# Layer 1's block products in three PSUM chains per half, read between the products

## The chip, the cores and the metric

One core of a Trainium2 chip runs the whole kernel in one launch. The metric is device time in microseconds (us), lower is better. The core's engines work side by side, each on its own instruction queue in order: TensorE (PE) multiplies matrices into PSUM banks, VectorE (DVE), ScalarE (ACT) and GpSimd (POOL) do element work, and SyncE (SP) issues transfers (DMA). An instruction waits until the semaphores it names have been raised by others, and everything queued behind it on its engine waits too.

## The reference

Three stages follow each other: attention with a decay, a mixture of 8 experts over its output, and a two-layer network with a leaky activation.

```python
x = attention(q, k, v, f)          # 4 x 8 heads, 576 tokens, 64 wide -> (2304, 512)

# mixture of experts: N, D, E, F = 2304, 512, 8, 1024
P = exp(x @ w_gate - max); 8 times: rows and columns of P are normalised
for e in range(E):
    h = np.maximum(x @ w1[e], 0.0)
    out += P[:, e:e + 1] * (h @ w2[e])

# two layers: d_model, d_ff = 512, 2048
h = x @ w_in
return np.maximum(0.01 * h, h) @ w_out
```

## The kernel before

**Stages.** Up to about 388 us the kernel does attention, with parts of the first experts mixed in, and the normalisation of the gate. From then on a main loop runs over 56 *groups* (`keys`). The 2304 tokens are three *parts* of 768, and the hidden width is cut in groups of 512 columns: 16 for the experts (g 0 to 15, two per expert), 4 for the last two layers (g 16 to 19). Part 0 begins at g 4, then come parts 1 and 2 with 16 groups each, then four groups of the last layers for each part.

**Precision.** Each float32 operand is split into a high half (`wh`, `xh`, `hh`), rounded by ACT, and a low half (`wl`, `xl`, `hl`), the rest by subtraction. Weights' low halves are GpSimd's (`w_split`, L202). A product is three matmuls, high by high, high by low and low by high.

**Layer 1.** A group's x @ w is done by a fast scheme with seven block products in place of eight, in two *halves* s = 0, 1 of 128 hidden columns each per block. The blocks of x (`b11` to `b22`) and of w (`a11` to `a22`) enter by sums and differences: `t1` to `t4` of x are made once per part, `s1` to `s4` of w in each group (`w1_events`: `s1` is an addition on DVE, L940, the `sub` are subtractions, L944, both working on the weights' buffer `wr`). A product (`prod`, L1027 to L1029) is six matmuls of 384 columns into a PSUM bank of its own, from a pool `ps1` of five. The output blocks are sums of products: c11 = p1 + p2; with u2 = p1 + p6 and u3 = u2 + p7: c22 = u3 + p5, c21 = u3 + p4, c12 = u2 + p5 + p3. ACT copies p1 and p5 from PSUM to SBUF (`keep`, L1034). DVE adds c11, u2, u3, c12 and c21 (L1044), GpSimd adds v = p5 + u2 and c22 = p5 + u3 (L1044, tiles `v` and `p`). c11 and u2 lie in one tile, `ct`. Then each c is made into its high half on ACT (`high`, L1062) and its low half on DVE (`low`, L1067 and, in the last layers, after a leaky activation, L1048, by L1070).

**Layer 2.** For the group before, six blocks l of 128 tokens each, twelve matmuls of 512 columns (L1130 to L1132) into another pool of three banks; DVE adds each to the sum over experts, weighted by the gate (`l2_add`, L1144). Scaling of the sums of the first experts at the loop's start is L1210.

**Order.** The program is a list of events with planned times (`at`); all events are sorted by time, after their `need` has put each behind those it depends on, and issued in that order. So the plan sets the order on every engine; the chip sets the times. `STEP_T` holds corrections to planned times, in the first group for every step. The products of a half come as p1 p6 p5 p2 p7 p3 p4 (`SET`). A pattern of 20 letters mixes products (p) and layer-2 blocks (l): `PAIRS` in the second and third group and the last, with the blocks in three runs, `THREES` in the 52 others, with two runs of three. The first group has products alone. `op_events` makes the operands of x anew at five turns, from one part to the next and at the groups of the last layers (`OPS` lists name, place, planned times of load, high and low half, and the engine of the low half, L823). Weights of a group come by two transfers, issued when the buffers `wr` are free.

Of the kernel before, what the change touches and what calls it, by code (L numbers as in the profile page):

```python
# [8 lines left out]
F32 = mybir.dt.float32  # L9
# [3 lines left out]
AF = mybir.ActivationFunctionType  # L13
ALU = mybir.AluOpType
# [121 lines left out]
def moe_kernel(ctx, tc, qT, kT, v, fg, w_gate, w1, w2, w_in, w_out, out):  # L136
# [192 lines left out]
    with ExitStack() as actx:  # L329
# [366 lines left out]
        def at(n, t, fn, *args):  # L696
            todo.append((n + t, len(todo), fn, args))
# [71 lines left out]
    fps[0] = ps2  # L769
    HB = 2 * KC - 1  # L770
    ht = late.tile([P, 2 * HB, TB], F32R, tag="xp", name="ht")
    ct = late.tile([P, 2, TB], F32, tag="xq", name="ct")
    hpb, owner, l2done = list(range(HB)), {}, set()


# [100 lines left out]
    def op_load(key, name, place):  # L876
# [136 lines left out]

    HT = {}

    def l1_events(prev, key, s, fin):

        part, g = key
        ps, tmp = {}, {}

        def prod(name, wn, xn):
            o = ps1.tile([P, 512], F32, tag="l1", name="ps1")[:, :TB]
            hi, lo = W1[key][wn]
            xh, xl = xo[xn]
            fs = slice(s * P, (s + 1) * P)
            for k in range(2):
                nc.tensor.matmul(o, hi[:, k, fs], xh[:, k, :], start=(k == 0), stop=False)  # L1027
                nc.tensor.matmul(o, hi[:, k, fs], xl[:, k, :], start=False, stop=False)  # L1028
                nc.tensor.matmul(o, lo[:, k, fs], xh[:, k, :], start=False, stop=(k == 1))  # L1029
            ps[name] = o  # L1030

        def keep(name):
            tmp[name] = tp.tile([P, TB], F32, tag=name, name=name, bufs=2 if name == "p1" else 1)
            nc.scalar.activation(tmp[name], ps.pop(name), AF.Copy)  # L1034

        def add(name, a, b, eng, into=None):
            a = ps.pop(a) if a in ps else tmp[a]
            if into:
                tmp[name] = tmp[into]
            elif name in ("c11", "u2"):  # L1040
                tmp[name] = ct[:, int(name == "u2"), :]
            else:
                tmp[name] = tp.tile([P, TB], F32, tag=name, name=name)
            eng.tensor_tensor(tmp[name], a, tmp[b], ALU.add)  # L1044

        def leaky(name):
            c = tmp[name]
            nc.scalar.activation(c, c, AF.Prelu, alpha=0.01)  # L1048

        def high(name, fh, th):  # L1050
            if th:
                hh = hpa.tile([P, TB], F32R, tag="hh", name="hh")
                hl = hpa.tile([P, TB], F32R, tag="hl", name="hl")
            else:
                i = hpb.pop(0)

                assert i not in owner or (owner[i], TPB - 1) in l2done, (key, owner[i])
                owner[i] = key
                hpb.append(i)
                hh, hl = ht[:, 2 * i, :], ht[:, 2 * i + 1, :]  # L1060
            tmp[fh, th] = (hh, hl)
            nc.scalar.activation(hh, tmp[name], AF.Relu if g < GE else AF.Copy)  # L1062

        def low(name, fh, th):
            hh, hl = HT.setdefault(key, {})[fh * 2 + s, th] = tmp[fh, th]
            if g < GE:
                nc.vector.scalar_tensor_tensor(  # L1067
                    hl, tmp[name], 0.0, f(hh), ALU.max, ALU.subtract)
            else:
# [21 lines left out]
        r11 = max(r1, fin["p2"]) + 0.5 + HOP
        last = (key, 0) if s else (prev, 1) if prev else None
        before = [(last[0], f"{last[1]} low c11")] if last else []
        at(r11 - 0.5, key, f"{s} c11", add, "c11", "p2", "p1", v,
           need=[(key, f"{s} keep p1"), (key, f"{s} p2"), *before])
        out_events("c11", 0, 0, r11)
        ru = max(r1, fin["p6"]) + 0.5 + HOP
        before = [(last[0], f"{last[1]} {n}") for n in ("v", "u3")] if last else []
        at(ru - 0.5, key, f"{s} u2", add, "u2", "p6", "p1", v,
           need=[(key, f"{s} keep p1"), (key, f"{s} p6"), *before])  # L1100
        step(fin["p5"] + HOP, "keep p5", keep, "p5", need=["p5"])
        r5 = fin["p5"] + 0.4 + HOP
        rv = max(r5, ru) + 1.0 + HOP
# [6 lines left out]
        out_events("c22", 1, 1, r22 + (LATE if g >= GE or g == GE - 1 and s else 0.0))  # L1110
        r3 = max(rv, fin["p3"]) + 0.5 + HOP
        step(r3 - 0.5, "c12", add, "c12", "p3", "v", v, "v", need=["v", "p3"])
        out_events("c12", 0, 1, r3)
        r4 = max(r22, fin["p4"]) + 0.5 + HOP
        step(r4 - 0.5, "c21", add, "c21", "p4", "u3", v, "u3", need=["c22", "p4"])
        out_events("c21", 1, 0, r4)
# [148 lines left out]
    for ki, key in enumerate(keys):  # L1265
# [130 lines left out]
```

## Time and profile before

| | us |
|---|---|
| median of the runs | 2147.82 |
| lowest, highest | 2146.76, 2148.51 |
| span of the profiled execution | 2145.7 |
| PE busy | 2111.3 |
| DVE busy | 1703.4 |
| POOL busy | 1374.1 |
| ACT busy | 1023.9 |

The span is from the first to the last instruction of one profiled execution. Busy is the time in which an engine works on an instruction; where one engine is busy all the time, the others' idle time costs nothing. The page has further the span in 40 slices, the groups of instructions by source line with their mean time, and the chain of waits that ended last. The trace behind it gives the same for any stretch: waits of an engine with what released them, and every instruction with its start.

### The profile page before, as it was taken

What the parts mean: (1) busy time and instruction counts of PE and PEld (TensorE: products, weight loads), DVE (VectorE), ACT (ScalarE), POOL (GpSimd) and SP (SyncE); (2) the same over time, 40 slices, a digit from 0 to 9 for tenths busy, and PEclk for the clock granted to TensorE, in tenths of its full rate; (3) what the DMA queues carried; (4) which work ended last, traced back from release to release, by engine and by line L of the source; (5) the groups of instructions that cost most, each with busy time, mean ns of one, the idle gap of its engine ahead of it and who ended that gap; (6) DMA issues with size and microseconds to landing.
All of it is one profiled execution on the core that took longest, in us unless ns stands there. A gap on an engine that the chain in (4) does not pass through costs nothing.

```text
span 2145.7 us, 31647 instructions
## 1 busy us (share of the span) xinstructions
PE 2111.3 (98%) x11134; PEld 1899.7 (89%) x11134; DVE 1703.4 (79%) x2545; ACT 1023.9 (48%) x2291; POOL 1374.1 (64%) x1039
## 2 busy tenths in 40 slices
PE   7999999999999999999999999999999999999999
PEld 6888888889999998999999998999999998989988
DVE  6799975788888877888888877888888885766754
ACT  7888863443334343333434353343434346554642
POOL 4666653776666677666656666665666576676662
PEclk9999999999999999999999999999999999999999
DMA  4555523323232324223222323223222233332310
GB/s 133 169 154 146 143 86 108 123 94 98 91 101 89 130 99 145 91 91 105 85 96 94 125 77 133 96 82 99 91 91 99 91 123 104 135 106 101 110 61 30
DMA packets 128063, 226.75 MB, mean 106 GB/s; under 512 B 11968, under 2 KB 45504, under 8 KB 127904
## 3 DMA queue, kind: packets, MB, share of 16 engines
q1 hardware_dynamic: 127904, 224.73, 32.6%
q8 instruction: 88, 1.44, 0.3%
q14 instruction: 71, 0.58, 0.1%
HBM read 189.24 MB, written 30.70 MB: 103 GB/s over the span
## 4 chain that ended last, share of the span: by engine, by line
PE 91%; DVE 5%; issue 1%; ACT 1%; POOL 1%; DMA 1%; SPq 0%; DVEq 0%; POOLq 0%; ACTq 0%
PE ps L1131 14%; PE ps L1132 14%; PE ps L1130 14%; PE ps L1027 12%; PE ps L1029 12%; PE ps L1028 12%; PE ps_pv L570 3%; PE ps L241 3%; PE ps L267 2%; PE ps_t L534 2%; PE ps_s L482 1%; PE ps_s L483 1%; POOL wl L202 1%; DVE ptl L550 1%; DMA wr<-in_w_dram 0%
## 5 line engine op out<-in xcount | busy, mean ns | idle before, releaser
L202 POOL TENSOR_TENSOR wl<-wr,wh 128x512 fp32r<-128x512 f32 x608 | 873.6, 1449 | 394.0 <-ACT wh L201 286.1
L201 ACT ACTIVATE wh<-wr 128x512 fp32r<-128x512 f32 x608 | 362.6, 621 | 461.7 <-DVE wr L944 243.9
L1027 PE MATMUL ps<-xh_t,wh 128*128 128x384 f32 x896 | 301.4, 336 | 3.5 <-DVE u L1044 2.3
L1029 PE MATMUL ps<-xh_t,wl 128*128 128x384 f32 x896 | 300.9, 336 | 0.0
L1028 PE MATMUL ps<-xl_t,wh 128*128 128x384 f32 x896 | 300.1, 335 | 0.0
L1044 POOL TENSOR_TENSOR p<-p,u 128x384 f32<-128x384 f32 x112 | 134.3, 1199 | 252.2 <-DVE u L1044 247.8
L1131 PE MATMUL ps<-wl,hh 128*128 128x512 f32 x672 | 262.6, 391 | 0.4 <-POOL wl L202 0.4
L1132 PE MATMUL ps<-wh,hl 128*128 128x512 f32 x672 | 262.7, 391 | 0.0
L1132 PE MATMUL ps<-wh,ht 128*128 128x512 f32 x672 | 262.6, 391 | 0.0
L1131 PE MATMUL ps<-wl,ht 128*128 128x512 f32 x672 | 262.4, 391 | 0.0
L1130 PE MATMUL ps<-wh,hh 128*128 128x512 f32 x672 | 262.0, 390 | 0.0
L1130 PE MATMUL ps<-wh,ht 128*128 128x512 f32 x672 | 262.0, 390 | 0.0
L1027 PE MATMUL ps<-xh_b,wh 128*128 128x384 f32 x672 | 224.8, 335 | 1.0 <-DVE v L1044 1.0
L1029 PE MATMUL ps<-xh_b,wl 128*128 128x384 f32 x672 | 224.6, 334 | 0.1
L1028 PE MATMUL ps<-xl_b,wh 128*128 128x384 f32 x672 | 224.5, 334 | 0.0
L1144 DVE SCALAR_TENSOR_TENSOR acc<-ps,prob,acc 128x512 f32<-128x512 f32 x252 | 184.7, 744 | 35.5 <-PE ps L1132 35.4
L1027 PEld LDWEIGHTS ps<-xh_t,wh 128*128 128x128 f32 x896 | 168.2, 188 | 8.8 <-DVE u L1044 3.2
L1062 ACT ACTIVATE hh<-v 128x384 fp32r<-128x384 f32 x112 | 58.5, 522 | 241.3 <-DVE v L1044 241.3
L1028 PEld LDWEIGHTS ps<-xl_t,wh 128*128 128x128 f32 x896 | 168.2, 188 | 4.1
L1029 PEld LDWEIGHTS ps<-xh_t,wl 128*128 128x128 f32 x896 | 168.1, 188 | 0.3 <-POOL wl L202 0.3
L1132 PEld LDWEIGHTS ps<-wh,ht 128*128 128x128 f32 x672 | 126.1, 188 | 26.5
L1132 PEld LDWEIGHTS ps<-wh,hl 128*128 128x128 f32 x672 | 126.1, 188 | 26.5
(177 smaller groups left out, 4649.4 us busy)
## 6 DMA issues: line engine op xcount, KB each, us to landing
wr<-in_w_dram SPq DMA_DIRECT2D x200, 512.0 KB
wr<-wf SPq DMA_DIRECT2D x48, 512.0 KB
rq<-in_qT_dram SPq DMA_DIRECT2D x64, 144.0 KB
rk<-in_kT_dram SPq DMA_DIRECT2D x64, 144.0 KB
cv<-in_w_in_dram SPq DMA_DIRECT2D x32, 256.0 KB
wf<-cv SPq DMA_DIRECT2D x64, 128.0 KB
cv<-in_w_out_dram SPq DMA_DIRECT2D x32, 256.0 KB
xt<-xr SPq DMA_DIRECT2D x20, 384.0 KB
```

The source lines that it names most:

```text
L201: nc.scalar.activation(hv, src, AF.Copy)
L202: nc.gpsimd.tensor_tensor(lv, src, f(hv), ALU.subtract)
L241: nc.tensor.matmul(ps, w_[:, fs], x_[k][:, xs], start=(x == 0), stop=(x == 11))
L570: nc.tensor.matmul(ps[:, a - ra:rb - ra], vp, s[:KV[j], o:o + rb - a], start=(x == 0), stop=(x == len(todo) - 1))
L1027: nc.tensor.matmul(o, hi[:, k, fs], xh[:, k, :], start=(k == 0), stop=False)
L1028: nc.tensor.matmul(o, hi[:, k, fs], xl[:, k, :], start=False, stop=False)
L1029: nc.tensor.matmul(o, lo[:, k, fs], xh[:, k, :], start=False, stop=(k == 1))
L1044: eng.tensor_tensor(tmp[name], a, tmp[b], ALU.add)
L1130: nc.tensor.matmul(ps, hh[:, ts], hi, start=(c == 0), stop=False)
L1131: nc.tensor.matmul(ps, hh[:, ts], lo, start=False, stop=False)
L1132: nc.tensor.matmul(ps, hl[:, ts], hi, start=False, stop=(c == FC - 1))
L1144: nc.vector.scalar_tensor_tensor(a, ps, pe, a, ALU.mult, ALU.add)
```

## The change

A half's seven products go into three banks that stay open: chain A takes p1 and p2, B takes p6, p7 and p4, C takes p5 and p3. Only a chain's first product starts it (`start`); the later ones add to what lies there. Between products the bank is read: k1 (copy of p1, on ACT) from A; u2 = B + k1, u3 = B + k1 and c21 = B + k1 from B after p6, p7 and p4; c22 = C + u3 and c12 = C + u2 from C after p5 and p3. c11 is A itself; its high and low half read PSUM. Of a half's work the additions c11 and v and the copy of p5 are gone, and c22 is now DVE's. The products p2, p7, p3 and p4 have a `need` on the read before them (k1, u2, c22, u3). The tile `ct` is gone; k1, u2 and u3 have two buffers each.

The order of products is a new table for both halves together (a digit for the half, one for the product), one for the first group and one for the others, and one pattern with layer 2's blocks in runs of three, two and one in all groups. The corrections of `STEP_T` for the first group's additions and halves are gone. In `OPS` the operand t3 takes the place of b11 and is loaded and split ahead of b21.

```diff
-    ("b21", "b21", None, -8.4, -6.6, "v"),
-    ("t3", "b11", -9.0, -2.5, 0.0, "p"),
+    ("t3", "b11", -12.0, -8.4, -6.6, "p"),
+    ("b21", "b21", None, -1.5, 0.5, "v"),
...
+    CHAIN = dict(p1="A", p2="A", p6="B", p7="B", p4="B", p5="C", p3="C")
...
         def prod(name, wn, xn):
-            o = ps1.tile([P, 512], F32, tag="l1", name="ps1")[:, :TB]
+            ch = CHAIN[name]
+            if ch not in ps:
+                ps[ch] = ps1.tile([P, 512], F32, tag="l1", name="ps1")[:, :TB]
+            o = ps[ch]
+            first, last = name in ("p1", "p6", "p5"), name in ("p2", "p4", "p3")
...
-                nc.tensor.matmul(o, hi[:, k, fs], xh[:, k, :], start=(k == 0), stop=False)
...
-            nc.scalar.activation(tmp[name], ps.pop(name), AF.Copy)
...
+                nc.tensor.matmul(o, hi[:, k, fs], xh[:, k, :], start=first and k == 0, stop=False,
+                                 skip_group_check=True)
...
+        def keep():
+            tmp["k1"] = tp.tile([P, TB], F32, tag="k1", name="k1", bufs=2)
+            nc.scalar.activation(tmp["k1"], ps["A"], AF.Copy)
...
-            eng.tensor_tensor(tmp[name], a, tmp[b], ALU.add)
+                tmp[name] = tp.tile([P, TB], F32, tag=name, name=name, bufs=2)
+            nc.vector.tensor_tensor(tmp[name], ps[ch], tmp[b], ALU.add)
...
+            if name == "c11" and g < GE:
+                tmp[name] = ps["A"]
...
+        after = {"p2": ["k1"], "p7": ["u2"], "p3": ["c22"], "p4": ["u3"]}
         for name in SET:
-            at(fin[name] - TPROD, key, f"{s} {name}", prod, name, WN[name], XN[name])
+            at(fin[name] - TPROD, key, f"{s} {name}", prod, name, WN[name], XN[name],
+               need=[(key, f"{s} {n}") for n in after.get(name, ())])
...
-        step(rv - 1.0, "v", add, "v", "p5", "u2", p, need=["keep p5", "u2"])
-        step(r22 - 1.0, "c22", add, "c22", "p5", "u3", p, "p5", need=["v", "u3"])
+        step(r2 - 0.5, "u2", add, "u2", "B", "k1", need=["k1", "p6"])
+        step(r3 - 0.5, "u3", add, "u3", "B", "k1", need=["u2", "p7"])
+        step(r22 - 0.5, "c22", add, "c22", "C", "u3", "u3", need=["u3", "p5"])
+        step(r12 - 0.5, "c12", add, "c12", "C", "u2", "u2", need=["c22", "p3"])
+        step(r21 - 0.5, "c21", add, "c21", "B", "k1", "k1", need=["u3", "p4"])
...
-    PAIRS, THREES = "pppllpppppllpppppllp", "pppplllppppppplllppp"
-    SET = ["p1", "p6", "p5", "p2", "p7", "p3", "p4"]
+    ORDER = "01 06 05 07 02 11 03 04 16 15 17 12 13 14".split()
+    FIRST_ORDER = "01 06 05 11 07 02 16 03 04 15 17 12 13 14".split()
+    PATTERN = "ppplllpppppppllpplpp"
+    SET = ["p1", "p6", "p5", "p7", "p2", "p3", "p4"]
```

What this does to the order of instructions is shown at three places. The first is DVE's queue in the first group, from the addition s1 of the next group's weights on (`s1`, `wr`: weights; `u3`, `ct`, `v`: sums of products; `ht`, `hl`: low halves). Before:

```order
L940 TENSOR_TENSOR s1_5530<-wr_5501,wr_5503 128x512
L1044 TENSOR_TENSOR v_5524<-ps1_5537,v_5524 128x384
L1044 TENSOR_TENSOR u3_5545<-ps1_5516,ct_4931 128x384
L1067 SCALAR_TENSOR_TENSOR ht_4930<-ct_4931,ht_4930 128x384
L944 TENSOR_TENSOR wr_5501<-wr_5501 128x2x256
L944 TENSOR_TENSOR wr_5501<-s1_5530,wr_5501 128x2x256
L1044 TENSOR_TENSOR u3_5545<-ps1_5553,u3_5545 128x384
L1067 SCALAR_TENSOR_TENSOR hl_5570<-p5_5495,hh_5569 128x384
L1044 TENSOR_TENSOR ct_4931<-ps1_5588,p1_5586 128x384
```

After (c22 is the second addition into `u3`; `u2_5574` is u2 of half 1; c12 and c21 are the additions into `u2_5493` and `k1`):

```order
L927 TENSOR_TENSOR s1_5526<-wr_5499,wr_5501 128x512
L1036 TENSOR_TENSOR u3_5538<-ps1_5469,k1_5476 128x384
L931 TENSOR_TENSOR wr_5499<-wr_5499 128x2x256
L1036 TENSOR_TENSOR u3_5538<-ps1_5486,u3_5538 128x384
L931 TENSOR_TENSOR wr_5499<-s1_5526,wr_5499 128x2x256
L1064 SCALAR_TENSOR_TENSOR ht_4930<-ps1_5450,ht_4930 128x384
L1064 SCALAR_TENSOR_TENSOR hl_5560<-u3_5538,hh_5559 128x384
L1036 TENSOR_TENSOR u2_5574<-ps1_5542,k1_5520 128x384
L1036 TENSOR_TENSOR u2_5493<-ps1_5486,u2_5493 128x384
L931 TENSOR_TENSOR wr_5501<-wr_5501,wr_5499 128x2x256
L1036 TENSOR_TENSOR k1_5476<-ps1_5469,k1_5476 128x384
```

The addition c22, for which p3 now waits, stands behind s1, u3 and one subtraction, and a second and a third subtraction stand ahead of the additions of half 1.

The second place is DVE's queue in the second group, from its s1 on (`acc`: sums of layer 2's blocks; `xr`: x). Before:

```order
L940 TENSOR_TENSOR s1_5749<-wr_5713,wr_5715 128x512
L1144 SCALAR_TENSOR_TENSOR acc4_96<-ps2_5731,prob_104,acc4_96 128x512
L944 TENSOR_TENSOR wr_5713<-wr_5713 128x2x256
L1044 TENSOR_TENSOR ct_4931<-ps1_5759,p1_5684 128x384
L826 TENSOR_TENSOR xr_5581<-xr_5581 128x2x384
L1044 TENSOR_TENSOR u3_5789<-ps1_5768,ct_4931 128x384
L1067 SCALAR_TENSOR_TENSOR ht_4930<-ct_4931,ht_4930 128x384
L944 TENSOR_TENSOR wr_5713<-s1_5749,wr_5713 128x2x256
L1044 TENSOR_TENSOR v_5723<-ps1_5782,v_5723 128x384
L1044 TENSOR_TENSOR u3_5789<-ps1_5794,u3_5789 128x384
```

After:

```order
L927 TENSOR_TENSOR s1_5729<-wr_5699,wr_5701 128x512
L1129 SCALAR_TENSOR_TENSOR acc4_96<-ps2_5711,prob_104,acc4_96 128x512
L931 TENSOR_TENSOR wr_5699<-wr_5699 128x2x256
L813 TENSOR_TENSOR xr_5576<-xr_5576 128x2x384
L931 TENSOR_TENSOR wr_5699<-s1_5729,wr_5699 128x2x256
L1129 SCALAR_TENSOR_TENSOR acc5_97<-ps2_5739,prob_104,acc5_97 128x512
L1036 TENSOR_TENSOR u3_5773<-ps1_5662,k1_5669 128x384
L1036 TENSOR_TENSOR u3_5773<-ps1_5676,u3_5773 128x384
L931 TENSOR_TENSOR wr_5701<-wr_5701,wr_5699 128x2x256
L1064 SCALAR_TENSOR_TENSOR ht_4930<-ps1_5652,ht_4930 128x384
```

The pair u3 and c22 of half 0 comes behind the third acc addition of the group; before, u3 (out of `ct`) stood ahead of the second subtraction, and c22 was not in this queue. In later groups the order around it is the same, here of a group of part 1:

```order
L1129 SCALAR_TENSOR_TENSOR acc0_92<-ps2_9606,prob_104,acc0_92 128x512
L1129 SCALAR_TENSOR_TENSOR acc1_93<-ps2_9623,prob_104,acc1_93 128x512
L1036 TENSOR_TENSOR u3_9655<-ps1_9586,k1_9570 128x384
L1036 TENSOR_TENSOR u3_9655<-ps1_9596,u3_9655 128x384
L1064 SCALAR_TENSOR_TENSOR ht_4930<-ps1_9550,ht_4930 128x384
L1064 SCALAR_TENSOR_TENSOR hl_9670<-u3_9655,hh_9669 128x384
```

The third place is GpSimd's queue in the first group (`wl`: low halves of weights). Before:

```order
L202 TENSOR_TENSOR wl1_5483<-wr_5458,wh1_5482 128x512
L202 TENSOR_TENSOR wl1_5498<-wr_5460,wh1_5497 128x512
L1044 TENSOR_TENSOR v_5524<-p5_5495,ct_4931 128x384
L202 TENSOR_TENSOR wl0_5527<-wr_5501,wh0_5526 128x512
L202 TENSOR_TENSOR wl1_5534<-wr_5458,wh1_5533 128x512
L1044 TENSOR_TENSOR p5_5495<-p5_5495,u3_5545 128x384
L202 TENSOR_TENSOR wl0_5561<-wr_5503,wh0_5560 128x512
L202 TENSOR_TENSOR wl0_5566<-wr_5501,wh0_5565 128x512
L202 TENSOR_TENSOR wl0_5614<-wr_5501,wh0_5613 128x512
L1044 TENSOR_TENSOR v_5627<-p5_5617,ct_4931 128x384
```

After:

```order
L190 TENSOR_TENSOR wl1_5481<-wr_5457,wh1_5480 128x512
L190 TENSOR_TENSOR wl1_5496<-wr_5459,wh1_5495 128x512
L190 TENSOR_TENSOR wl0_5523<-wr_5499,wh0_5522 128x512
L190 TENSOR_TENSOR wl1_5529<-wr_5457,wh1_5528 128x512
L190 TENSOR_TENSOR wl0_5551<-wr_5501,wh0_5550 128x512
L190 TENSOR_TENSOR wl0_5556<-wr_5499,wh0_5555 128x512
L190 TENSOR_TENSOR wl0_5563<-wr_5499,wh0_5562 128x512
```

The additions v and c22 (`p5`) are no longer between the weights' low halves.

## Rows read from the trace of the kernel before

**Rows 1.** The page: span, and busy time of each engine with its share.
```profile
span 2145.7 us, 31647 instructions
...
PE 2111.3 (98%) x11134; PEld 1899.7 (89%) x11134; DVE 1703.4 (79%) x2545; ACT 1023.9 (48%) x2291; POOL 1374.1 (64%) x1039
```

**Rows 2.** Busy us by window: window, length, the engines, PEclk, DMA share.
```profile
500.00:600.00 100.00, 100.00 (x510) 91.33 (x509) 87.00 (x115) 40.23 (x84) 64.31 (x49) 1.00 0.30 95
```

**Rows 3.** PE's waits from 420 us on: releaser, us in total, times, longest.
```profile
PE ps L1027 <- DVE v L1044: 1.0, 1, 1.0
PE ps L1131 <- POOL wl L202: 0.4, 1, 0.4
```

**Rows 4.** PE's waits from 350 to 450 us.
```profile
PE ps L241 <- DVE acc L273: 2.4, 1, 2.4
PE ps L1027 <- DVE u L1044: 2.3, 1, 2.3
PE ps L1027 <- DVE v L1044: 2.1, 2, 1.1
```

**Rows 5.** Groups by line: count, busy us, mean ns, idle before and its releaser.
```profile
L1044 DVE TENSOR_TENSOR ct<-ps,p 128x384 f32<-128x384 f32 x224 | 115.5, 546 | 4.2 <-PE ps L1029 4.0
L1067 DVE SCALAR_TENSOR_TENSOR ht<-ct,ht 128x384 fp32r<-128x384 f32 x88 | 106.6, 1211 | 48.5 <-ACT ht L1062 48.0
...
L823 DVE TENSOR_TENSOR xl_t<-xr,xh_t 128x768 fp32r<-128x768 f32 x18 | 27.4, 1520 | 3.5 <-ACT xh_t L819 3.5
...
L1044 POOL TENSOR_TENSOR p<-p,u 128x384 f32<-128x384 f32 x112 | 134.3, 1199 | 252.2 <-DVE u L1044 247.8
...
L1034 ACT ACTIVATE p<-ps 128x384 f32<-128x384 f32 x224 | 107.1, 478 | 21.0 <-PE ps L1029 19.7 <-DVE hl L1067 1.1
```

**Rows 6.** Timeline of PE: start, us, instruction; first product, then mid-run.
```profile
388.52 0.33 PE L1027 MATMUL ps<-xh_b,wh 128*128 128x384 f32 x1
...
1006.30 0.39 PE L1130 MATMUL ps<-wh,hh 128*128 128x512 f32 x1
...
1008.38 0.39 PE L1130 MATMUL ps<-wh,hh 128*128 128x512 f32 x1
...
1010.42 0.39 PE L1130 MATMUL ps<-wh,hh 128*128 128x512 f32 x1
...
1014.50 0.33 PE L1027 MATMUL ps<-xh_t,wh 128*128 128x384 f32 x1
...
1015.57 0.33 PE L1027 MATMUL ps<-xh_b,wh 128*128 128x384 f32 x1
...
1016.61 0.33 PE L1027 MATMUL ps<-xh_t,wh 128*128 128x384 f32 x1
```

**Rows 7.** Timeline of DVE, first group, with idle before and releaser.
```profile
392.06 1.33 DVE L1210 SCALAR_TENSOR_TENSOR acc<-acc,prob,acc 128x512 f32<-128x512 f32 x1
...
395.88 1.42 DVE L940 TENSOR_TENSOR s<-wr 128x512 f32<-128x512 f32 x1 [2.02 <-DMA wr<-in_w_dram]
...
398.80 1.50 DVE L944 TENSOR_TENSOR wr<-wr 128x512 f32<-128x512 f32 x1
400.40 1.57 DVE L944 TENSOR_TENSOR wr<-s,wr 128x512 f32<-128x512 f32 x1
```

**Rows 8.** The chain that ended last, 380 to 450 us: start, us, what.
```profile
389.70 6.06 DMA wr<-in_w_dram
...
415.05 3.59 POOL wl L202 x2
418.65 4.37 DMA wr<-in_w_dram
```

**Rows 9.** Busy time by window: after the gaps of rows 4.
```profile
375.00:376.00 1.00, 1.00 (x5) 1.00 (x4) 0.93 (x2) 0.70 (x3) 0.36 (x1) 0.50 0.00 0
...
403.00:406.00 3.00, 3.00 (x19) 3.00 (x18) 3.00 (x5) 1.54 (x4) 1.41 (x2) 1.00 0.93 341
```

More of the change, by code (lines that the diff above doesn't have):

```diff
@@ L771, in moe_kernel @@
     ht = late.tile([P, 2 * HB, TB], F32R, tag="xp", name="ht")
-    ct = late.tile([P, 2, TB], F32, tag="xq", name="ct")
     hpb, owner, l2done = list(range(HB)), {}, set()
@@ L1026, in prod, with add @@
             for k in range(2):
-                nc.tensor.matmul(o, hi[:, k, fs], xh[:, k, :], start=(k == 0), stop=False)
[L1028 to L1033, printed above, removed]
-            nc.scalar.activation(tmp[name], ps.pop(name), AF.Copy)
-        def add(name, a, b, eng, into=None):
-            a = ps.pop(a) if a in ps else tmp[a]
+                nc.tensor.matmul(o, hi[:, k, fs], xh[:, k, :], start=first and k == 0, stop=False,
+                                 skip_group_check=True)
+                nc.tensor.matmul(o, hi[:, k, fs], xl[:, k, :], start=False, stop=False,
+                                 skip_group_check=True)
+                nc.tensor.matmul(o, lo[:, k, fs], xh[:, k, :], start=False, stop=last and k == 1,
+                                 skip_group_check=True)
+        def keep():
+            tmp["k1"] = tp.tile([P, TB], F32, tag="k1", name="k1", bufs=2)
+            nc.scalar.activation(tmp["k1"], ps["A"], AF.Copy)
+        def add(name, ch, b, into=None):
             if into:
                 tmp[name] = tmp[into]
-            elif name in ("c11", "u2"):
-                tmp[name] = ct[:, int(name == "u2"), :]
-            else:
-                tmp[name] = tp.tile([P, TB], F32, tag=name, name=name)
-            eng.tensor_tensor(tmp[name], a, tmp[b], ALU.add)
+            else:
+                tmp[name] = tp.tile([P, TB], F32, tag=name, name=name, bufs=2)
+            nc.vector.tensor_tensor(tmp[name], ps[ch], tmp[b], ALU.add)
         def leaky(name):
-            c = tmp[name]
-            nc.scalar.activation(c, c, AF.Prelu, alpha=0.01)
+            if name == "c11":
+                tmp[name] = tp.tile([P, TB], F32, tag="u2", name="c11", bufs=2)
+                nc.scalar.activation(tmp[name], ps["A"], AF.Prelu, alpha=0.01)
+            else:
+                nc.scalar.activation(tmp[name], tmp[name], AF.Prelu, alpha=0.01)
         def high(name, fh, th):
@@ L1074, in step, with out_events @@
             return t
-        def out_events(name, fh, th, ready):
-            need = name
+        def out_events(name, fh, th, ready, need):
             if g >= GE:
@@ L1090, in l1_events @@
         r1 = fin["p1"] + 0.4 + HOP
[L1091 to L1103, printed above, removed]
-        step(rv - 1.0, "v", add, "v", "p5", "u2", p, need=["keep p5", "u2"])
-        r7 = max(ru, fin["p7"]) + 0.5 + HOP
-        step(r7 - 0.5, "u3", add, "u3", "p7", "u2", v, need=["u2", "p7"])
-        r22 = max(r7, rv) + 1.0 + HOP
@@ L1108, in l1_events @@
-        step(r22 - 1.0, "c22", add, "c22", "p5", "u3", p, "p5", need=["v", "u3"])
[L1110 to L1116, printed above, removed]
+        step(r1 - 0.4, "k1", keep, need=["p1"])
@@ new lines, in l1_events @@
+        r2 = max(r1, fin["p6"]) + 0.5 + HOP
+        step(r2 - 0.5, "u2", add, "u2", "B", "k1", need=["k1", "p6"])
+        r3 = max(r2, fin["p7"]) + 0.5 + HOP
+        step(r3 - 0.5, "u3", add, "u3", "B", "k1", need=["u2", "p7"])
+        r22 = max(r3, fin["p5"]) + 0.5 + HOP
+        step(r22 - 0.5, "c22", add, "c22", "C", "u3", "u3", need=["u3", "p5"])
+        out_events("c22", 1, 1, r22, "c22")
+        out_events("c11", 0, 0, fin["p2"], "p2")
+        r12 = max(r22, fin["p3"]) + 0.5 + HOP
@@ L1118, in moe_kernel @@
+        step(r12 - 0.5, "c12", add, "c12", "C", "u2", "u2", need=["c22", "p3"])
+        out_events("c12", 0, 1, r12, "c12")
+        r21 = max(r3, fin["p4"]) + 0.5 + HOP
+        step(r21 - 0.5, "c21", add, "c21", "B", "k1", "k1", need=["u3", "p4"])
+        out_events("c21", 1, 0, r21, "c21")
     l2ps = {}
@@ L1223, in moe_kernel @@
     GROUP = 14 * TPROD + 6 * TL2
-    PAIRS, THREES = "pppllpppppllpppppllp", "pppplllppppppplllppp"
-    SET = ["p1", "p6", "p5", "p2", "p7", "p3", "p4"]
+    ORDER = "01 06 05 07 02 11 03 04 16 15 17 12 13 14".split()
+    FIRST_ORDER = "01 06 05 11 07 02 16 03 04 15 17 12 13 14".split()
+    PATTERN = "ppplllpppppppllpplpp"
+    SET = ["p1", "p6", "p5", "p7", "p2", "p3", "p4"]
     WN = dict(p1="a11", p2="a12", p3="s4", p4="a22", p5="s1", p6="s2", p7="s3")
     XN = dict(p1="b11", p2="b21", p3="b22", p4="t4", p5="t1", p6="t2", p7="t3")
-    def mixed(s, l):
-        p = [(s, x) for x in SET]
-        return p[0:3] + l[0:1] + p[3:5] + l[1:2] + p[5:6] + l[2:3] + p[6:7]
     t = 0.0
@@ L1269, in moe_kernel @@
         if ki == 0:
-            q = mixed(0, []) + mixed(1, [])
+            q = [(int(x[0]), "p" + x[1]) for x in FIRST_ORDER]
         else:
             L = [("l", i) for i in (3, 4, 5, 0, 1, 2)]
-            products = [(s, x) for s in range(2) for x in SET]
-            q = [products.pop(0) if x == "p" else L.pop(0) for x in (PAIRS if ki < 3 or not nxt else THREES)]
+            products = [(int(x[0]), "p" + x[1]) for x in ORDER]
+            q = [products.pop(0) if x == "p" else L.pop(0) for x in PATTERN]
             if prev[1] == GE - 1:
@@ L1341, in moe_kernel @@
     for j, i in enumerate((3, 4, 5, 0, 1, 2)):
-        l2_events(base + TL2 * j, "end", keys[-1], i)
+        l2_events(base + 1.6 + TL2 * j, "end", keys[-1], i)
     when = {(key, name): t for t, _, key, name, _, _, _ in todo}
@@ L1382 @@
     }
-    nc = _bacc.Bacc("TRN2", target_bir_lowering=False, num_devices=1)
+    nc = _bacc.Bacc("TRN2", target_bir_lowering=False, num_devices=1, dynamic_dma_scratch_size=1024)
     arrays, args = {}, []
```

2 lines of the change are left out of this document (removed), and 12 rows, old and new, of the table STEP_T.

## The prediction, made before the changed kernel was run

> **What bounds the kernel now.** First the page's busy shares: TensorE (PE) works for 98% of the span, VectorE (DVE) 79%, GpSimd (POOL) 64%, ScalarE (ACT) 48%; the span is 2145.7 us and the median of the runs 2147.82, so 2.1 us lie outside the span [rows 1]. An average hides where PE is idle, so next the busy times by window: 100 us of the main loop show PE busy for all 100 at clock 1.00 [rows 2]. There PE is the bound, and what other engines save is worth nothing. Third, PE's waits with what released them: from 420 us on two are left, 1.0 and 0.4 us [rows 3]; the stretch from 350 to 450 adds, at layer 1's matmuls, one of 2.3 and one of 1.1 (its two of 2.1 together include the 1.0) [rows 4]. So the main loop loses 2.3 + 2.1 + 0.4 = 4.8 us, all in its first groups, and nothing after 450 us. No relief beside PE can win more than that. PE's own work stays: the same products, as many matmuls of the same shapes.
>
> **Work taken off.** Gone per half group (112 halves) are a DVE addition (c11, 546 ns), an ACT copy (478 ns) and GpSimd's addition v; c22 moves from GpSimd (1199 ns) to DVE (546, as the other additions from PSUM) [rows 5]. That relieves GpSimd of 2 x 112 x 1.2 = 269 us and ACT of 112 x 0.478 = 54; DVE comes out even. All of it lies under a PE that does not wait: 0 us after 450 us. If the cover went, another engine would show 100; DVE with 87 of 100 us [rows 2] is nearest and gets no more work.
>
> **Waits added.** Four products per half now go into a bank that is read in between: p2 waits for the ACT copy, p7 for u2, p3 for c22, p4 for u3. Each costs what its reader is late. Between p7's end and p3's start in half 0 the order sets two products, 2 x 1.04 = 2.08 us (six matmuls from 1015.57 to 1016.61 [rows 6]). In it u3 and c22 run on DVE, 2 x 0.55, and 0.4 goes to the drain of p7's last matmul and to handing over. About 0.6 us of slack are left; the other pairs have another product or a layer-2 block between them. In the middle of the run DVE's instruction ahead of u3 is the acc addition of the block that ends as p7 begins, done about as p7 ends. I take 0 for these groups; the bound above stands with the rivals.
>
> A rule of the Trainium skill speaks against the change: "PSUM — Partial Sum Buffer", section "Summary: rules for kernel authors", tells a kernel that reads PSUM while a matmul runs to aim the matmul at a different bank. A bank for each product is what the kernel before has, and rows 3 and 4 agree that this leaves PE no wait after 450 us. By the rule each of the eight returns per group is a risk, and its time is that of the second rival.
>
> **The first group (+4.6).** No layer-2 blocks cover it. Products start every 1.04 us from 388.52 [rows 6]. Half 0's p7 is fifth and could start at 392.7; it needs u2, which stands on DVE behind an acc scaling of 1.33 us begun at 392.06 [rows 7]: u2 from 393.3 to 393.85, a wait of 1.1. Then p3 could start at 397.0. It needs c22, and DVE's order is s1, u3, a subtraction, c22. s1 waits for weights, whose transfer began at 389.70 [rows 8], and runs from 395.88 for 1.42 us; u3 ends at 397.8, the subtraction of 1.50 at 399.3, c22 at 399.85 [rows 7]: 2.9. Half 1's p7 could start at 403.0; its u2 stands behind another subtraction (1.57 [rows 7]) and two low halves (0.55 to 1.2 [rows 5]), done at about 403.4: 0.4. Half 1's p3 could start at 405.6 and needs c22 behind c12, a third subtraction (about 1.5), c21, two low halves and u3, done at about 408.1: 2.5. Together 1.1 + 2.9 + 0.4 + 2.5 = 6.9, against 2.3 before [rows 4]. Bounds: +1.7 without the two waits of half 1 (short low halves, no third subtraction ahead), +5.1 with long ones.
>
> **The second and third group (+1.2, -0.4).** Here c22 of half 0 comes behind s1, two acc additions, three steps of 0.7 to 1.5 and u3: some 5.9 us after s1 begins. s1 waits for weights whose transfer of 4.37 us is issued when GpSimd has split those before [rows 8]. GpSimd now lacks up to 2.8 us of additions ahead of that, so s1 comes at 420.3 to 423.1. PE, later by 4.6, wants p3 at about 425.3; c22 is done at 426.2 to 429.0: a wait of 0.9 to 3.7 against 2.1 before [rows 4], so -1.2 to +1.6. I take +1.2, since the splits also wait until PE frees older weights. The 0.4 in the third group [rows 3] goes.
>
> **The clock (0).** A PE gap of 2.4 us before layer 1 [rows 4] was followed by a window at 0.50, half the clock; after the gap of 2.3 the granted clock was 1.00 [rows 9]. The new waits reach 3.7. I take nothing, and 3 us (twice the 1.5 lost in 3 us at half clock) as the upper bound.
>
> **The order (+3.6).** From the fourth group on, 52 groups have layer 2 in two blocks now and in three after. Nine matmuls from a block's first start take 1006.30 to 1008.38, 2.08, the next nine 2.04: +0.04. Back in layer 1 the first six take 1014.50 to 1015.57, 1.07, the next 1.04: +0.03 [rows 6]. A block more costs 0.07, and 52 x 0.07 = 3.6. Bounds 2.6 to 4.7, by rounding of 0.01 in each of the two.
>
> **Turns of the parts (+1.5).** Five times x's operands are made anew; t3 is now loaded and split earlier, and a low half of 1520 ns on DVE [rows 5] can stand ahead of u3 and c22 against a slack of 0.6, so up to 0.9 a turn. Before, no wait is there [rows 3]. I take 0.3 each; bounds 0 to 4.5.
>
> **Sum:** 2145.7 + 4.6 + 1.2 - 0.4 + 3.6 + 1.5 = 2156.2 us of span, and with 2.1 outside it 2158.3, +0.5%.
>
> **The rivals.**
> - *No dearer start.* The waits of the first groups only change their names (from u and v to c22), and only the switches are left: 2147.8 + 3.6 = 2151.4, +0.17%. For it: the same weight transfers [rows 8] stand ahead of both. Against it: c22 stands behind a whole subtraction, in the one group that nothing covers.
> - *A wait in every group.* If DVE is late for half 0's p3 by 0.5 us on the mean in 52 groups, +26: 2184. It decides from anything over 0.6 us placed just ahead of u3. For it: DVE at 87 of 100 us, and low halves of 1211 ns. Against it: the order puts there only the acc addition that ends with p7.
> - *Faster.* GpSimd's 269 us are what the first groups lacked: weights come earlier, the 4.8 us go, and switches cost nothing new because the matmuls' spacing is set elsewhere: 2147.8 - 4.8 = 2143.0, -0.22%. It decides from where s1 no longer leads the waits. Against it: the transfer behind 395.88 began at 389.70 [rows 8], when one product had run, and up to there both programs are the same.
> - *It doesn't do what it says* (the copies that vanish come back as waits of the same length in every group): that is the second rival's time.
>
> **How the numbers follow.** The forecast has 0.62, no dearer start 0.18, a wait in every group 0.13, faster 0.07. A measurement can tell about 0.2%, 4.3 us. Of the faster case I count 0.01 as within: faster 0.06, within 0.19 (the rest from no dearer start), slower 0.75. The range begins at the no-dearer case, 2151. Above, the bounds add 0.5 + 0.4 (start), 1.1 (switches), 3.0 (turns) and 3 (clock), 8 us in all: 2166.3; with a mean wait of 0.07 us in the steady groups it is 2170, and the larger waits are left out.
>
> **What would show it.** After: waits of PE at layer 1 in the first two groups, released by DVE's additions, some 7 us in the first; 100 of 100 us busy in the middle; 0.04 and 0.03 us at each change of shape, once more per group; GpSimd some 269 us less busy. The forecast is wrong if windows of the middle show PE under 100, if a product takes other than 1.04 us, if the clock falls in the main loop, or if s1 does not start at about 395.9.

## The result, and the profile after

The changed kernel takes 2159.67 us (median; 2157.15 to 2161.65), the kernel before 2147.29 beside it: a ratio of 1.0058, 95% interval 1.0044 to 1.0073. It is slower, by 12.4 us in the medians; 2158.3 was forecast. The profiled execution is the fastest of the four, 2157.15, with a span of 2155.3 against 2145.7 [rows 1], 9.6 us more.

The page, first the span, then busy time and share of each engine; below it, busy time by window in the form of [rows 2]:

```profile
span 2155.3 us, 30954 instructions
...
PE 2115.7 (98%) x11134; PEld 1901.5 (88%) x11134; DVE 1515.8 (70%) x2545; ACT 972.5 (45%) x2179; POOL 1083.7 (50%) x815
```

```profile
390.00:400.00 10.00, 6.64 (x34) 6.00 (x34) 8.05 (x10) 4.36 (x9) 7.20 (x5) 0.93 0.55 188
400.00:410.00 10.00, 8.52 (x44) 8.20 (x43) 8.33 (x14) 5.34 (x11) 6.10 (x5) 0.90 0.52 191
...
500.00:600.00 100.00, 100.00 (x505) 90.69 (x504) 74.34 (x117) 35.87 (x75) 49.10 (x36) 1.00 0.27 87
...
2000.00:2100.00 100.00, 99.03 (x497) 89.30 (x496) 59.92 (x87) 49.57 (x101) 47.99 (x35) 1.00 0.27 87
```

VectorE is rid of 187.6 us (1703.4 to 1515.8), GpSimd of 290, ScalarE of 51, and the time is longer: in the middle TensorE is busy for 100 of 100 us as before, and it is idle only at the start and at two places near the end. The waits of TensorE, from 386 to 460 us and from 460 on, answer to [rows 3, 4]:

```profile
PE ps L1020 <- DVE u L1036: 8.3, 4, 3.5
PE ps L1024 <- POOL wl L190: 0.2, 1, 0.2
```

```profile
PE ps L1020 <- DVE u L1036: 1.9, 2, 1.0
```

So 8.5 us up to 460 us against 4.8 before, and 1.9 at two places after it. All but 0.2 us are released by a sum on VectorE, as forecast. Where they lie and what follows each is in TensorE's timeline (start, us, instruction, idle before it with its releaser):

```profile
393.18 0.44 PE L1020 MATMUL ps<-xh_t,wh 128*128 128x384 f32 x1 [0.92 <-DVE u L1036]
...
399.05 0.69 PE L1020 MATMUL ps<-xh_b,wh 128*128 128x384 f32 x1 [2.44 <-DVE u L1036]
399.53 0.52 PE L1022 MATMUL ps<-xl_b,wh 128*128 128x384 f32 x1
399.85 0.52 PE L1024 MATMUL ps<-xh_b,wl 128*128 128x384 f32 x1
...
407.35 0.45 PE L1020 MATMUL ps<-xh_b,wh 128*128 128x384 f32 x1 [1.48 <-DVE u L1036]
...
427.68 0.41 PE L1020 MATMUL ps<-xh_b,wh 128*128 128x384 f32 x1 [3.51 <-DVE u L1036]
...
1898.89 0.44 PE L1020 MATMUL ps<-xh_b,wh 128*128 128x384 f32 x1 [0.98 <-DVE u L1036]
```

They are half 0's p7 and p3 and half 1's p3 in the first group, half 0's p3 in the second, and half 0's p3 at a turn to the last layers (the same again at 2024). After 399.05 the matmuls start 0.32 apart in place of 0.17: half the clock, for nine matmuls, some 1.3 us. Windows behind the waits of 2.44 and 3.51, in the form of [rows 2], give the granted clock:

```profile
399.00:402.00 3.00, 2.95 (x9) 2.96 (x10) 2.36 (x4) 1.56 (x3) 1.67 (x2) 0.50 1.01 393
427.70:430.70 3.00, 3.00 (x17) 3.00 (x18) 2.51 (x6) 1.85 (x5) 1.29 (x1) 1.00 0.00 0
```

By the starts of matmuls, of which both traces hold all 8736 of the loop, the loop takes 10.9 us more from its first product to its last matmul: 4.5 up to the fourth group (3.7 of waits and 1.3 of half clock, less some small gaps that before has there and after has not), 3.5 in the changes of shape, spread evenly, 1.9 at the two turns, and about 1 in steps of at most 0.5 elsewhere. The span grew by only 9.6, since in this execution the loop starts 1.1 us sooner, at 387.43 in place of 388.52. The execution of before had waited 2.4 us ahead of the loop and then run at half the clock [rows 4, 9], and this one did neither. The change has no part in that: four of the changed kernels below show the half clock at that place again.

### The profile page after: what moved, and what is told of

Read it like the earlier page. It is cut to its first block, busy times and chain, and to the rows that moved or that the text cites. A ratio compares the mean times of both kernels' runs of the same rounds, so it can differ in the third digit from the quotient of the medians.

```text
span 2155.3 us, 30954 instructions
## 1 busy us (share of the span) xinstructions
PE 2115.7 (98%) x11134; PEld 1901.5 (88%) x11134; DVE 1515.8 (70%) x2545; ACT 972.5 (45%) x2179; POOL 1083.7 (50%) x815
## 4 chain that ended last, share of the span: by engine, by line
PE 92%; DVE 5%; issue 1%; ACT 1%; POOL 1%; DMA 0%; SPq 0%; DVEq 0%; POOLq 0%; ACTq 0%
PE ps L1117 14%; PE ps L1116 14%; PE ps L1115 14%; PE ps L1020 12%; PE ps L1024 12%; PE ps L1022 12%; PE ps_pv L558 3%; PE ps L229 2%; PE ps L255 2%; PE ps_t L522 2%; PE ps_s L470 1%; PE ps_s L471 1%; DVE wr L931 1%; POOL wl L190 1%; DVE ptl L538 0%
## 5 line engine op out<-in xcount | busy, mean ns | idle before, releaser
L190 POOL TENSOR_TENSOR wl<-wr,wh 128x512 fp32r<-128x512 f32 x608 | 832.6, 1392 | 804.2 <-ACT wh L189 481.7
L189 ACT ACTIVATE wh<-wr 128x512 fp32r<-128x512 f32 x608 | 349.2, 623 | 264.2 <-DVE wr L931 255.2
L1059 ACT ACTIVATE hh<-u 128x384 fp32r<-128x384 f32 x224 | 116.9, 522 | 223.7 <-DVE u L1036 223.0
L1059 ACT ACTIVATE ht<-ps 128x384 fp32r<-128x384 f32 x88 | 43.3, 492 | 360.1 <-PE ps L1024 360.1
L1036 DVE TENSOR_TENSOR u<-ps,k 128x384 f32<-128x384 f32 x224 | 124.0, 554 | 52.9 <-PE ps L1024 50.2
L190 POOL TENSOR_TENSOR wl<-s,wh 128x512 fp32r<-128x512 f32 x56 | 86.4, 1543 | 137.9 <-ACT wh L189 137.9
```

Source lines behind the costliest of these rows:

```text
L189: nc.scalar.activation(hv, src, AF.Copy)
L190: nc.gpsimd.tensor_tensor(lv, src, f(hv), ALU.subtract)
L1036: nc.vector.tensor_tensor(tmp[name], ps[ch], tmp[b], ALU.add)
```

## The experiments

**The wait of the first group moved.** One planned time, so that u3 and c22 stand ahead of s1 on VectorE.

```diff
-    ("first", "w1 1"): 0.89,
+    ("first", "w1 1"): 2.60,
```

> Changed kernel with one planned time moved: in the first group u3 and c22 of half 0 stand ahead of s1 on VectorE. Theory A (every wait at a layer-1 product is a cost of its own): the wait of 2.4 us at half 0's p3 goes and with it the half clock after it (1.3 us), so 3.8 us less than the changed kernel, about 2155.5. Theory B (VectorE's work of the first group is one chain, s1, subtractions, low halves, sums): the wait comes back at the products of half 1, whose u2 and c22 then stand behind s1 and the subtractions; the third group starts at most 1.3 us earlier, about 2158.

Measured: 2159.40 us, 1.0060 (1.0048 to 1.0073), no gain. The waits of TensorE from 386 to 460 us:

```profile
PE ps L1020 <- DVE u L1036: 6.7, 4, 3.6
PE ps L1020 <- DVE ht L1064: 1.2, 1, 1.2
PE ps L1024 <- POOL wl L190: 0.2, 1, 0.2
```

The wait of 2.44 at p3 is gone, and 1.19 (on a low half, which frees a bank for half 1's p5) and 1.12 (on u2, for half 1's p7) have come, so theory B holds in the first group: VectorE's queue is one chain there, and moving one step moves the wait. The waits are 0.4 us less in sum, which the time doesn't show.

**The wait of the second group.** Two subtractions put behind u3 and c22.

```diff
+        if key == keys[1]:
+            return "second"
...
+    ("second", "w1 4"): 4.50, ("second", "sum t3"): 5.00,
```

> Changed kernel with two planned times moved: in the second group the second subtraction and a subtraction of x stand behind u3 and c22 of half 0, not ahead. Theory A: c22 is done 2.6 us earlier, the wait of 3.5 us at half 0's p3 shrinks to about 0.9, nothing takes its place, since the weights of the third group have a layer-2 run more to come: 2.7 us less, and the runs about 4 us above the others (lower mean clock) vanish, if they come from a clock that falls after this wait: all runs within 1.5 us near 2155. Theory B: the weights of the third group come late instead, wait for wait, about 2159.

Measured: 2154.65 us (2153.93 to 2156.35), 1.0035 (1.0023 to 1.0048), 5 us less than the changed kernel. TensorE's wait there:

```profile
426.93 0.41 PE L1023 MATMUL ps<-xh_b,wh 128*128 128x384 f32 x1 [1.22 <-DVE u L1039]
```

1.22 in place of 3.51, and nothing in its place. Theory A holds where layer-2 blocks give the displaced work room. Of the 5 us the wait shows 2.3. The runs above the others are gone too: of the changed kernel's four, two had 2161 us at a mean clock of 0.997; of these five none has more than 2156.4, at 0.998 to 1.000. That agrees with a clock that falls, in some executions, after the long wait of the second group; the two runs themselves have no trace. The kernel of the experiment "The conversion moved", further down, has the same wait, and in its trace the clock does fall there. But the clock falls elsewhere too: the profiled execution here, the slowest of its five, has half the clock ahead of the loop, from 374 to 377 us, and after a wait of the first group. So how much of the difference the second group's wait made is not shown.

**The order of before with one more run of blocks.** The kernel before, with PAIRS in all groups.

```diff
-            q = [products.pop(0) if x == "p" else L.pop(0) for x in (PAIRS if ki < 3 or not nxt else THREES)]
+            q = [products.pop(0) if x == "p" else L.pop(0) for x in PAIRS]
```

> Kernel before with layer 2 in three runs of two blocks in all groups instead of two runs of three. Theory A: 52 more changes of shape each way at 0.04 and 0.03 us, 3.6 us more, about 2151; PE waits stay as they were. Rival: the changes of shape cost nothing by themselves, no difference from before (within 1 us).

Measured: 2150.10 us against 2146.68, 1.0014 (1.0005 to 1.0023): 3.4 us for 52 groups, 0.066 for a change of shape there and back. By the starts of the matmuls an ordinary group is 0.07 us longer, here as in the changed kernel. There is no wait of TensorE after 460 us, and up to there 4.3 us. The term of 3.6 is shown.

**Two runs of blocks on the chains.** The changed kernel without the third run, with an order of products that leaves three products between p7 and p3 of half 0.

```diff
+    ORDER2 = "01 06 05 07 02 11 16 03 04 15 17 12 13 14".split()
+    TWO = "ppplllppppppppplllpp"
...
-            products = [(int(x[0]), "p" + x[1]) for x in ORDER]
-            q = [products.pop(0) if x == "p" else L.pop(0) for x in PATTERN]
+            products = [(int(x[0]), "p" + x[1]) for x in (ORDER if ki < 3 or not nxt else ORDER2)]
+            q = [products.pop(0) if x == "p" else L.pop(0) for x in (PATTERN if ki < 3 or not nxt else TWO)]
```

> Changed kernel with layer 2 in two runs of three blocks from the fourth group on, and the order of products fitted to it (16 ahead of 03, 17 and 12 ahead of the second run), so that three products stand between p7 and p3 of half 0 and a run of blocks between those of half 1. Theory A: the chains cost nothing here, only the 52 changes of shape each way go: 3.6 us less than the changed kernel, about 2156. Rival: waits on the chains come in the middle of the run, PE below 100 of 100 us, and the time is no less or more.

Measured: 2181.32 us, 1.0159 (1.0145 to 1.0173): 22 us more, the rival. The waits after 460 us, then TensorE at one of them, then VectorE ahead of it:

```profile
PE ps L1020 <- DVE u L1036: 18.5, 32, 1.1
```

```profile
1009.73 0.44 PE L1020 MATMUL ps<-xh_t,wh 128*128 128x384 f32 x1 [0.56 <-DVE u L1036]
```

```profile
1005.57 0.29 DVE L993 TENSOR_SCALAR cv<-cv 128x256 uint32<-128x256 uint32 x1
1005.89 0.43 DVE L994 SCALAR_TENSOR_TENSOR cv<-cv 128x256 uint32<-128x256 uint32 x1
1006.35 1.43 DVE L995 SCALAR_TENSOR_TENSOR cv<-cv 128x256 uint32<-128x256 uint32 x1
1007.88 1.33 DVE L998 SCALAR_TENSOR_TENSOR cv<-cv 128x256 f32<-128x256 f32 x1
1009.13 0.54 DVE L1036 TENSOR_TENSOR u<-ps,k 128x384 f32<-128x384 f32 x1
```

Half 1's p7 waits for u2, which stands behind a conversion of weight bits, 3.5 us in a row; these belong to other work and occur in 32 groups, and there are 31 such waits of 0.56 and one of 1.1 elsewhere. By the starts of the matmuls the product begins 0.72 late, the first two after the wait stand further apart too, and a group with such a wait takes 0.84 more than the same group without it.

**The conversion moved.** The same kernel, and the first conversion of a group behind u2 of half 1.

```diff
-                k, tj = k0 + j, fin[j, "p2"] + 1.4
+                k, tj = k0 + j, (fin[1, "p6"] + 0.9 if j == 0 else fin[1, "p2"] + 1.4)
```

> As the changed kernel with two runs of three blocks and the fitted order, and the first conversion of weight bits of a group put behind u2 of half 1 on VectorE, not ahead of it. Theory A: the 32 waits in the middle of that kernel came from the conversion alone and go (0.72 us each); what is left is the changed kernel without 52 changes of shape each way and without the two waits at the last layers' turns: 2159.7 - 3.5 - 2 = about 2154. Rival: with two runs the chains wait for something else in its place, PE stays below 100 of 100 us, 2165 or more.

Measured: 2154.53 us, 1.0033 (1.0021 to 1.0044), 27 us less than without the move, of which 31 waits at 0.84 make 26, and TensorE at 100 of 100 us:

```profile
1000.00:1100.00 100.00, 100.00 (x504) 90.55 (x503) 75.28 (x116) 35.63 (x72) 48.48 (x36) 1.00 0.30 93
```

After 460 us one wait of 1.1 is left; the two at the turns are gone. In the first two groups the engines' order is still the changed kernel's, and the waits there, with the clock behind the last, are these:

```profile
393.43 0.44 PE L1020 MATMUL ps<-xh_t,wh 128*128 128x384 f32 x1 [0.92 <-DVE u L1036]
...
398.07 0.45 PE L1020 MATMUL ps<-xh_b,wh 128*128 128x384 f32 x1 [1.22 <-DVE u L1036]
...
402.21 0.44 PE L1020 MATMUL ps<-xh_t,wh 128*128 128x384 f32 x1 [0.74 <-DVE u L1036]
...
406.96 0.44 PE L1020 MATMUL ps<-xh_b,wh 128*128 128x384 f32 x1 [2.39 <-DVE u L1036]
...
427.34 0.66 PE L1020 MATMUL ps<-xh_b,wh 128*128 128x384 f32 x1 [3.56 <-DVE u L1036]
```

```profile
427.00:430.00 3.00, 2.66 (x8) 2.69 (x9) 2.09 (x5) 1.42 (x3) 1.27 (x1) 0.50 0.00 0
```

The chains themselves cost nothing in the middle, with two runs or three, as long as no other work stands ahead of a sum that a product waits for.

**One product between p7 and p3.**

```diff
-    ORDER = "01 06 05 07 02 11 03 04 16 15 17 12 13 14".split()
+    ORDER = "01 06 05 07 02 03 11 04 16 15 17 12 13 14".split()
```

> Changed kernel with one product in place of two between p7 and p3 of half 0 (half 1's p1 comes after p3, from the second group on). Theory A: the time that u3 and c22 need after p7, about 1.5 us with drain and handing over, is 0.45 more than one product of 1.04: a wait of about 0.45 us at p3 in every one of 55 groups, 25 to 30 us more than the changed kernel, about 2187, and PE at 98 to 99 of 100 us in the middle. Rival: a product that goes back to a bank waits for nothing worth naming (slack well over 1 us): within 3 us of the changed kernel.

Measured: 2194.61 us, 1.0218 (1.0204 to 1.0232), 35 us more than the changed kernel. Waits after 460 us, and a window of the middle:

```profile
PE ps L1020 <- DVE u L1036: 18.5, 54, 2.0
```

```profile
1000.00:1100.00 100.00, 99.20 (x494) 88.68 (x493) 70.61 (x115) 34.60 (x72) 48.97 (x36) 1.00 0.28 89
```

A wait in every one of 54 groups, as theory A has it; in the ordinary ones TensorE is idle for 0.20, and the matmul starts 0.37 later than it would without one, so that u3 and c22 take 1.4 us, and the slack with two products is 0.67; the whole group takes 0.50 more. At the turns of parts the waits are longer, 0.4 to 2.0, and the second group's grew to 4.8: the total was 5 us over the upper end expected.

**GpSimd loaded again.** An addition per half into a tile of its own, its result unused.

```diff
+        def again():
+            nc.gpsimd.tensor_tensor(spare, tmp["u2"], tmp["k1"], ALU.add)
...
+        step(r2, "again v", again, need=["u2"])
```

> Changed kernel with an addition of 128x384 on GpSimd per half again, after u2, its result not used: GpSimd gets back 112 x 1.2 = 134 us of the 269. Theory A: it lies under a PE that is busy, 0 us after 450 us, and 0 to 2 us more in the first groups by later weights: 2159 to 2162. Rival: the relief of GpSimd was worth something in the middle of the run: 2165 or more, with waits of PE there.

Measured: 2168.02 us, 1.0092 (1.0077 to 1.0108), 8 us more: the rival's time, but with waits at the start and at turns alone and not throughout the middle. Waits of TensorE, up to 460 us and after:

```profile
PE ps L1021 <- DVE u L1037: 9.9, 4, 4.6
```

```profile
PE ps L1021 <- DVE u L1037: 7.0, 6, 1.6
```

Ordinary groups wait for nothing, but the start has 1.6 us more of waits and half the clock in three stretches in place of one, and six turns wait in place of two. What GpSimd does to VectorE shows in the mean times of two of VectorE's forms, first of the changed kernel, then of this one:

```profile
L1036 DVE TENSOR_TENSOR u<-ps,u 128x384 f32<-128x384 f32 x224 | 123.9, 553 | 11.2 <-PE ps L1024 7.5
...
L931 DVE TENSOR_TENSOR wr<-s,wr 128x512 f32<-128x512 f32 x56 | 43.7, 780 | 16.5 <-POOL wl L190 11.9
```

```profile
L1037 DVE TENSOR_TENSOR u<-ps,u 128x384 f32<-128x384 f32 x224 | 123.8, 553 | 12.2 <-PE ps L1025 8.4
...
L932 DVE TENSOR_TENSOR wr<-s,wr 128x512 f32<-128x512 f32 x56 | 75.8, 1353 | 15.5 <-POOL wl L190 10.5 <-DVE wr L932 0.5
```

An addition with an operand in PSUM takes 553 ns either way; a subtraction with both in SBUF takes 780 or 1353. It is the one form that changed so much: the other subtraction stays at 929 and 922 ns, and s1 goes from 1189 to 1067, since it matters which of VectorE's work the added one falls beside.

**A better order.** Two runs, the conversion moved, and sixteen planned times of the start and the first two groups, two of them as in the second experiment. The diff shows changed entries alone.

```diff
+    ("second", "w1 4"): 4.50, ("second", "sum t3"): 5.00, ("second", "w1 1"): 4.00, ("second", "sum t1"): -2.50,
+    ("first", "1 u2"): -1.60, ("first", "0 low c21"): 3.00, ("first", "0 low c22"): -2.30,
+    ("first", "0 c21"): -0.80, ("first", "1 u3"): -1.50,
...
-    ("first", "w1 1"): 0.89, ("first", "w1 2"): 1.29, ("first", "w1 3"): 1.45, ("first", "w1 4"): 1.33, ("first", "w1 6"): 2.47,
+    ("first", "w1 1"): 2.60, ("first", "w1 2"): 2.79, ("first", "w1 3"): 2.25, ("first", "w1 4"): 2.83, ("first", "w1 6"): 6.00,
...
-    ("start", "scale 2"): -2.11, ("start", "scale 5"): -5.40,
+    ("start", "scale 2"): -1.90, ("start", "scale 5"): -2.00,
```

> The two-run kernel with the conversion moved, and the VectorE queue of the first two groups put in another order by planned times: acc scalings behind u2, c22 of half 0 and u2 of half 1 ahead of s1, u3 and c22 of half 1 ahead of the third subtraction, in the second group s1 behind the three acc additions. Theory A (order on VectorE alone makes the start's waits): 3 to 4 us of waiting are left up to 460 us, no half clock, about 2144, 3 us less than before. Theory B (VectorE's work of the first group is the chain, in whatever order): the waits move to other products, 8 us are left, about 2149.

Measured: 2146.10 us against 2147.27, 0.9996 (0.9988 to 1.0005): level with the kernel before, 13.6 us under the changed one and 8.4 under the one with the conversion moved, from which it differs by planned times alone. Waits up to 460 us, and the clock after the longest:

```profile
PE ps L1031 <- DVE u L1047: 3.5, 3, 1.9
```

```profile
403.61 0.69 PE L1031 MATMUL ps<-xh_b,wh 128*128 128x384 f32 x1 [1.94 <-DVE u L1047]
404.10 0.52 PE L1033 MATMUL ps<-xl_b,wh 128*128 128x384 f32 x1
404.42 0.52 PE L1035 MATMUL ps<-xh_b,wl 128*128 128x384 f32 x1
```

Theory A by and large: the start's waits are a matter of VectorE's order, where the whole queue is put in order and not one step. The half clock that was to go is still there. It doesn't beat the kernel before by more than can be told.

## Why the prediction was right, point by point

- **What bounds the kernel.** Right: 100 of 100 us before and after; 187.6, 290 and 51 us less on three engines brought nothing in the middle. That VectorE "comes out even" was wrong: it lost 187.6 us, 156 of them in the low halves of c in the experts' groups (360 to 204 us), which take 0.55 us where no GpSimd instruction runs beside them. The last experiment but one shows the limit of "0 us": half of GpSimd's relief taken back costs nothing in ordinary groups and 8 us at the start and the turns. "0 us" held for the ordinary groups, not for the edges. There the relief had paid for a part of the chains' price, and without it the change would have cost more than 12 us.
- **The first group, +4.6.** The mechanism was right, the sizes were not. Of 1.1, 2.9, 0.4 and 2.5 the trace has 0.92, 2.44, none and 1.48: 4.8 and not 6.9, +2.5 against 2.3 before. Four of the experiments' kernels (the second, the two with two runs, and the one with one product between) have the same order up to there, and in their profiles the waits are 0.9 to 1.0, 1.2, 0.7 and 2.4, some 5.3 together: all four waits of the prediction, with only the second far off. The step that failed took the durations of VectorE from rows of before, where GpSimd was at work beside it. After:

```profile
395.08 1.77 DVE L927 TENSOR_TENSOR s<-wr 128x512 f32<-128x512 f32 x1 [1.95 <-POOL wl L190]
396.77 0.55 DVE L1036 TENSOR_TENSOR u<-ps,k 128x384 f32<-128x384 f32 x1
397.24 1.28 DVE L931 TENSOR_TENSOR wr<-wr 128x512 f32<-128x512 f32 x1
398.44 0.55 DVE L1036 TENSOR_TENSOR u<-ps,u 128x384 f32<-128x384 f32 x1
398.91 0.68 DVE L931 TENSOR_TENSOR wr<-s,wr 128x512 f32<-128x512 f32 x1
```

  The subtractions take 1.28 and 0.68 where [rows 7] had 1.50 and 1.57. And s1 starts at 395.08, not at about 395.9, which the prediction had named as a sign against itself. The loop's earlier start accounts for that: counted from the first product, s1 comes after 7.65 us, before after 7.36. The profile names GpSimd as what s1 waited for last; in the four other profiles it is the transfer, as forecast, here in that of the conversion moved:

```profile
394.73 1.12 DVE L927 TENSOR_TENSOR s<-wr 128x512 f32<-128x512 f32 x1 [1.35 <-DMA wr<-in_w_dram]
```

- **The second and third group, +1.2 and -0.4.** The wait is 3.51 (3.3 was meant) and lies where it was put; +1.4 and -0.4. The chain is as told: weights at 420.8, then s1, acc, subtractions, u3, c22. It takes 6.7 us where 5.9 was reckoned, and p3 could have started at 424.2, not at 425.3. The second experiment, which moves two of these steps, takes 2.3 us off the wait.
- **The clock, 0.** Wrong as a value, inside its bound: 1.3 us in the profiled execution, and the clock fell in the main loop, another of the prediction's signs against itself. Two of the other executions took some 4 us more at a lower mean clock, which lifts the median over the profile by 2.5 us; where it fell in them no trace shows. With the first group 2.1 cheaper, and the loop 1.1 early in the profile, this cancels: the total came right in part by luck.
- **The order, +3.6.** Right: 3.4 measured alone. That the third run is there for a reason was not said: without it, half 1's u2 falls behind the conversions, 22 us, unless these are moved.
- **The turns, +1.5.** 1.9 us of waits, but in two turns of 1.0 and none in the three others, so the trace agrees with the mechanism (a low half ahead of u3), with a subtraction of 1.78 beside it, and not with the spread; no run tries the low half alone. VectorE at the first:

```profile
1892.69 2.00 DVE L810 TENSOR_TENSOR xl_t<-xr,xh_t 128x768 fp32r<-128x768 f32 x1
1894.60 1.78 DVE L931 TENSOR_TENSOR wr<-wr 128x512 f32<-128x512 f32 x1
...
1897.69 0.55 DVE L1036 TENSOR_TENSOR u<-ps,k 128x384 f32<-128x384 f32 x1
1898.27 0.56 DVE L1036 TENSOR_TENSOR u<-ps,u 128x384 f32<-128x384 f32 x1
```

- **The steady groups, 0.** Right, with a slack of 0.67 where 0.6 was reckoned. The rival of a wait in every group was real, though not in this kernel: it is what one product less between p7 and p3, or a conversion in the wrong place, makes of it. What these runs show is that a bank that goes back to TensorE after a read costs what the reader is late, 0.50 us a group with one product between, and nothing where it is not late. The rule of the Trainium skill that the prediction weighed ("PSUM — Partial Sum Buffer", section "Summary: rules for kernel authors") asks for another bank while a read is under way and names no time for it; here the matmul waits until the read is done, so no run tests it.

What stays open is why the clock falls after some waits and not after others, and whether the changed kernel's slower executions have the half clock after the second group's wait, ahead of the loop, or both.

## What to carry to other kernels

Where TensorE is busy all the time, work saved on the other engines is worth nothing there by itself, and a change that pays for it with products that must wait for a read has mostly its own price: the spacing it needs in the order, here one more change of shape per group or a conversion moved out of the way, and waits wherever no layer-2 work covers the start. Reckon such a wait as the whole queue ahead of the reader on its engine; moving one step of a full queue only moves the wait. And take durations for a changed kernel from stretches in which the same neighbours are at work, since an engine relieved elsewhere can make this one faster.

## What the runs showed of the hardware

- VectorE's operations with both operands in SBUF take longer while a GpSimd instruction runs, those that read PSUM don't. In the trace of before, counted by starts and durations, the low half of 128x384 out of `p` and `hh` takes 0.55 us in the 42 instances that have no GpSimd instruction beside them and 1.66 on the mean in the 42 that lie wholly beside one; the sum out of PSUM and `ct` takes 0.56 and 0.55.
- A wait of TensorE costs more than its idle time: with 0.56 us of idle a group takes 0.84 more, with 0.20 it takes 0.50 more. The first matmul starts 0.72 and 0.37 late, and the next one 0.28 after it, before they are back at 0.17.
- After some waits the granted clock is 0.50 for a while, after others it stays at 1.00. It fell behind 2.44 us in the changed kernel's profile, 1.94 in the last kernel's, 3.56 with the conversion moved, 4.6 with GpSimd loaded and 3.7 in the first two-run kernel, which the window below shows. It stayed at 1.00 behind 3.51 in the changed kernel's profile and behind 2.3 before. The length of the wait alone doesn't tell.

```profile
432.00:437.00 5.00, 5.00 (x17) 5.00 (x17) 2.60 (x6) 1.99 (x5) 1.27 (x1) 0.50 0.00 0
```
